# First two scans of a fused scan and two-MLP kernel: the order of ScalarE's fillers, the start of the second substitution, and the queue that loads the first MLP's x

## The chip, the cores and the metric

One Trainium2 chip, one core. The metric is the time of one execution on the device in microseconds (us), the median of several runs.

## What is computed

The reference runs a linear-attention scan with a state of 40 by 40 for each of 4 batches and 8 heads over 768 steps, and feeds its output through two MLPs:

```python
for t in range(S):                                   # S = 768, state: B=4, H=8, 40 x 40
    y[:, :, t] = np.einsum('bhd,bhde->bhe', rt, state)
    Sa = np.einsum('bhde,bhe->bhd', state, at)
    state_decay = state * wt[:, :, None, :] - np.einsum('bhd,bhe->bhde', Sa, bt)
    state = state_decay + np.einsum('bhd,bhe->bhde', vt, kt)
...
h = x @ w_in                                         # x: 3072 x 320, w_in: 320 x 2048
g = np.maximum(h, 0.0) + alpha * np.minimum(h, 0.0)
x = g @ w_out
...
g = x @ w_gate                                       # 320 x 1536
silu = g * (1.0 / (1.0 + np.exp(-g)))
out = (silu * (x @ w_val)) @ w_out
```

The MLP weights arrive as 8-byte floating point and are cut down to pairs of 4-byte parts on the chip.

## The kernel before

The 768 steps are cut into 6 blocks `m` of 128 steps, and a block into 2 chunks of 64. A pair (block, batch) is an item; there are 24, four to a block. Each item goes through these stages, all of them Python generators that yield after each step:

- `preps` (7 steps to an item): decayed copies of the inputs on DVE (`kbt` L592, `AN` L579, the running products L565 to L572), products `mnp` on PE, whose results ScalarE copies into the block's triangular matrices `tt` (L610, L613) and into `AN` (L617). The matrices of even blocks are `tt_172`, of odd ones `tt_173`; the number is the buffer's.
- `inverse(m)` (40 steps, once to a block): the triangular inverse of all four items' matrices, the substitution. DVE transposes `tt` (L650), runs 31 rounds of a product (L665) and a subtraction (L673), and transposes back (L676, L678). PE then makes the off-diagonal quarter in two sets of small products, `eps` (L686) and `dps` (L705); between and behind them stand ScalarE copies (L698, L694, L713). L650 needs the last L613 of the block.
- `seq(i, ch)` (13 steps to an item): the scan. For each chunk: `zp` on PE (L769), `zs` copied by ScalarE (L771), `pp` (L779, which needs the block's inverse), copies `ut` and `pv` (L781, L783), transposes, copies `gs` and `s` (L793, L798), `gp` on PE (L802), a masking on DVE (L805), `yp` on PE (L817, L821), and on DVE the state (L825), the output (L829) and the next chunk's start (L746). Two items run side by side on two channels. At its end ScalarE's queue writes the output to DRAM, `xd` (L837).
- `conv1` (32 steps): conversion of the first MLP's weights: a load `raw` on SP's queue, ScalarE (L191, L192, L217), DVE (L193), GpSimd (L218), a store to `wd`.
- `mlp1(m)`: the first MLP over a block. It loads x from `xd` into `xa` in three tiles (`fill_x`; L319 twice, L323 for the two halves of the third), splits it into high and low parts (ScalarE L217 or L324, DVE L218 or L325), and goes through 16 blocks of weights, `f`: 8 up products `u` (L294), ScalarE and DVE for the activation (L334, L335, L217, L218), 8 down products `d` (L300 to L306). For block 0 the first 8 weight blocks run over half of x (items 0 and 1) before the rest.

`drive` takes steps from several of these by their progress and gives each a priority; a list scheduler then puts the instructions of the whole program in one fixed order for each engine. An engine runs its own order strictly, and so does a queue: an instruction whose semaphores are not there holds up all behind it. DMAs of SP and of ScalarE share 8 completion semaphores, and a DMA waits until the one before it on its semaphore has landed. `tc.issue_after(ins)` orders what is traced under it behind `ins` on the same engine; `lifted(n)` raises the priority by `n`. In `drive` the first `lead` generators log the last instruction of their step on each engine; of the others, those that `who` names have their instructions ordered behind that log on the engines that `engs` names.

The part around the change: `preps` of block 0, then `inverse(0)`, then a first `drive` with the scans of items 0 and 1, the remaining 27 steps of `preps` of block 1, all of `inverse(1)` and the last 20 steps of `conv1`; then a second one with the scans of items 2 and 3 and 17 steps of `mlp1(0)`; then a loop over the other blocks, in which block `m` is scanned while block `m + 1` is prepared and inverted and block `m - 1` goes through the first MLP. The second MLP stands at the end.

Of the kernel before, what the change touches and what calls it, by code (L numbers as in the profile page):

```python
# [16 lines left out]
FAC = 1.0  # L17
ALIAS = 1
XPRI = 1000
# [26 lines left out]
RA = 1.0  # L46
MP = 0
YB = 1
CP = 2000
# [14 lines left out]
L = 64  # L64
HALF = 32
LOOK = 2
TRB = 5
LATE = 20
XLEAD = 6
# [4 lines left out]
def kernel(  # L74
# [50 lines left out]
    @contextmanager  # L125
    def held_by(ins):
        n0 = len(traced())
        yield
        if ins is not None:
            for x in traced()[n0:]:  # L130
                if x.engine == nc.sync.engine:
                    tc.add_manual_dep(
                        x, ins.ins.name,
                        mybir.DependencyInfo(mybir.DependencyClass.Sync, mybir.DependencyReason.DATA),
                        reason="pace of loads",
                    )
# [39 lines left out]
    @contextmanager  # L176
    def lifted(n=XPRI):
        tc.cur_priority -= n
        yield
        tc.cur_priority += n  # L180
# [130 lines left out]
        xst = pool.tile([128, n], F32R, tag="xst", name="xst")  # L311
        return xh, xl, xst

    def fill_x(pool, xs, src, c0, c1):
        xh, xl, xst = (x[..., c0:c1] for x in xs)
        for j in range(3):
            xa = pool.tile([128, c1 - c0], F32, tag="xa", name="xa", bufs=XAB[0])
            if j < 2:
                nc.sync.dma_start(out=xa, in_=src[j * 128:j * 128 + 128])  # L319
                split(xa, xh[:, j], xl[:, j], nc.vector)  # L320
            else:
                for p in (lo, hi):
                    nc.sync.dma_start(out=xa[p], in_=src[256:DM])  # L323
                nc.scalar.copy(out=xst, in_=xa)  # L324
                nc.vector.tensor_tensor(out=xst[hi], in0=xa[hi], in1=xst[hi].bitcast(F32), op=ALU.subtract)  # L325

# [31 lines left out]
    def mlp1(j, early=0):  # L358
# [15 lines left out]
        seen = set()  # L374
        for f, c0, c1 in plan:
            if not seen & {(c0, c1), (0, half) if early and c0 == 0 else (c0, c1)}:
                with lifted(), held_by(ago(XLEAD) if j == NM - 1 else None):
                    b0, b1 = c0 // TB, c1 // TB
                    fill_x(xp1, xs, xd[j][:, b0:b1].rearrange("f b t -> f (b t)"), c0, c1)
                seen.add((c0, c1))  # L380
                yield
            t = fetch(wp1, 2 * f, True, j, done)
            ps = e1p["psu"].tile([128, c1 - c0], F32, tag="u", name="u")
            done.append(up_mm(ps, t, tuple(x[..., c0:c1] for x in xs)))
            yield
            if len(pend) == (2 if j == NM - 1 else DEP):
                down(*pend.pop(0))
            pend.append((f, c0, c1, *prelu(e1p["gp3"] if j == NM - 1 and fs.index(f) % 3 == 2 else gp1, ps, f, c1 - c0)))
            yield
# [514 lines left out]
    if FA == 0:  # L904
        drive(
            *((chain(seq(j, j), seq(j + 2, j)), 2 * N_SEQ, SP) for j in range(2)),
            (rest1, FAC * nrest, HP2),
            (take(c1, NC1), NC1 - EC - EC0, CP),
            lead=2, engs=G1, lag=LG1, who=W1,
        )  # L910
    else:
        drive(
            (seq(0, 0), N_SEQ, SP), (seq(1, 1), N_SEQ, SP),
            (take(rest1, int(nrest * RA)) if RA < 1 else rest1, FAC * nrest, HP2),
            (take(c1, NC1), NC1 - EC - EC0, CP),
        )
    boot.close()
    ps1 = ctx.enter_context(ExitStack())
# [7 lines left out]
    if FA:  # L926
        drive(
            (seq(2, 0), N_SEQ, SP), (seq(3, 1), N_SEQ, SP),
            (rest1, FAC * nrest * (1 - RA) + .1, HP2),
            (take(gms[0], 2 * FA + 1), 2 * FA + 1, MP),  # L930
        )
    for m in range(1, NM):
# [201 lines left out]
```

## Time and profile before

| | |
|---|---|
| median of 3 runs | 1228.72 us (1226.75 to 1228.92) |
| profiled execution | 1225.27 us, its span 1223.6 us |
| mean granted clock of TensorE | 0.952 of full speed |
| busy in the span | PE 1107.1 us (90%), PEld 935.2, DVE 735.3 (60%), ACT 607.1 (50%), POOL 272.0 |
| chain that ended last | PE 29% of the span, as far back as it is followed |

PE is TensorE's products, PEld its weight loads, DVE VectorE, ACT ScalarE, POOL GpSimd; SPq and ACTq are the queues that issue DMAs. Times in rows are us from the span's start unless marked ns. In a timeline row stand the start, the duration, the engine, the line, what it writes and reads, the form, how many equal ones are merged, and in brackets the idle time before it and what ended it. In a row of windows stand the stretch, its length, the busy time and in brackets the instructions of PE, PEld, DVE, ACT and POOL, the granted clock of TensorE, the busy share of the DMA engines and GB/s.

### The profile page before, as it was taken

To read this page: it belongs to the slowest core of one execution; us is meant where nothing else is said; L and a number is where in the kernel's file an instruction comes from. 1 tells how busy PE (TensorE), PEld (TensorE's weight loads), DVE (VectorE), ACT (ScalarE), POOL (GpSimd) and SP (SyncE) were. 2 spreads that over 40 slices of the span, in tenths; PEclk is the share of its full clock that TensorE was granted. 3 is DMA by queue.
4 is the path that set the end of the run, shared out by engine and by line. 5 is a ranking of instruction groups with operands and counts; after the bars stand their busy time and mean duration, and the time that the engine had idled before them with its cause. 6 is when DMAs were issued, how large, how long until landed. Compare 5 with 4: busy or idle time off the path is not lost. (4 is left out here: it accounts for less than half of the span.)

```text
span 1223.6 us, 24425 instructions
## 1 busy us (share of the span) xinstructions
PE 1107.1 (90%) x9098; PEld 935.2 (76%) x9098; DVE 735.3 (60%) x1592; ACT 607.1 (50%) x1514; POOL 272.0 (22%) x434
## 2 busy tenths in 40 slices
PE   4566678999999989899898999999999999999998
PEld 3345567877878778787686777788788888888887
DVE  7787897698499569859664434879532323223222
ACT  5769658645844764673654433555332323222222
POOL 8115333301212221521363000536300000000000
PEclk9659787999999999899989999999999999999999
DMA  4565697466454544545585473795010101010000
GB/s 145 179 198 176 210 310 228 138 200 185 132 170 137 170 140 148 181 133 147 160 269 189 129 221 135 261 351 158 1 48 1 48 1 48 2 39 9 22 1 21
DMA packets 94884, 166.35 MB, mean 136 GB/s; under 512 B 13232, under 2 KB 43184, under 8 KB 94768
## 3 DMA queue, kind: packets, MB, share of 16 engines
q1 hardware_dynamic: 86608, 160.88, 41.8%
q10 hardware_dynamic: 8160, 3.93, 1.1%
q8 instruction: 72, 1.18, 0.4%
q14 instruction: 44, 0.36, 0.1%
HBM read 136.98 MB, written 27.79 MB: 135 GB/s over the span
## 5 line engine op out<-in xcount | busy, mean ns | idle before, releaser
L217 ACT CAST gh<-g 128x512 fp32r<-128x512 f32 (+1 forms) x176 | 105.5, 600 | 165.0 <-DVE g L1070 115.9
L218 DVE TENSOR_TENSOR gl<-g,gh 128x512 fp32r<-128x512 f32 (+1 forms) x176 | 124.2, 706 | 89.5 <-ACT gh L217 87.1
L1070 DVE TENSOR_TENSOR g<-pv,sg 128x512 f32<-128x512 f32 x72 | 49.8, 691 | 206.3 <-PE pv L294 201.6
L294 PE MATMUL u<-xh,wt 128*128 128x512 f32 (+1 forms) x416 | 147.4, 397 | 11.9 <-DVE g L335 11.0
L335 DVE SCALAR_TENSOR_TENSOR g<-g,neg,u 128x512 f32<-128x512 f32 (+1 forms) x104 | 72.8, 702 | 70.4 <-ACT g L334 69.8
L294 PEld LDWEIGHTS u<-xh,wt 128*128 128x128 f32 x416 | 79.7, 194 | 31.4 <-DVE g L335 14.3
L1068 ACT ACTIVATE sg<-pg 128x512 f32<-128x512 f32 x72 | 43.1, 598 | 121.1 <-PE pg L294 121.1
L294 PE MATMUL pg<-xh,w 128*128 128x512 f32 x288 | 102.5, 394 | 0.0
L294 PE MATMUL pv<-xh,w 128*128 128x512 f32 x288 | 100.4, 389 | 0.0
L334 ACT ACTIVATE g<-u 128x512 f32<-128x512 f32 (+1 forms) x104 | 58.6, 564 | 82.7 <-PE u L294 69.9
L1054 PE MATMUL o<-w,gh 128*128 128x320 f32 x288 | 87.5, 309 | 2.6 <-ACT gh L217 2.6
L1055 PE MATMUL o<-w,gh 128*128 128x320 f32 x288 | 87.8, 309 | 0.0
L301 PE MATMUL d<-gl,wt 128*128 128x512 f32 (+1 forms) x208 | 83.2, 402 | 2.2 <-DVE gl L218 2.2
L604 PE MATMUL mnp<-AN,kbt 128*128 128x128 f32 x384 | 60.1, 307 | 25.6 <-DVE AN L579 13.6
L665 DVE TENSOR_TENSOR tmp<-la 128x96 f32<-128x96 f32 (+43 forms) x306 | 79.5, 286 | 2.7 <-POOL la L653 0.7
L294 PE MATMUL u<-xl,wt 128*128 128x512 f32 (+1 forms) x208 | 80.2, 385 | 0.0
L302 PE MATMUL d<-gh,wt 128*128 128x512 f32 (+1 forms) x208 | 79.9, 386 | 0.0
L1056 PE MATMUL o<-w,gl 128*128 128x320 f32 x288 | 77.2, 310 | 1.0 <-DVE gl L218 0.9
L673 DVE TENSOR_TENSOR la<-la,tmp 128x96 f32<-128x96 f32 (+43 forms) x306 | 76.8, 277 | 2.0
L760 POOL COPY gs<-raw_v 64x160 f32<-64x160 f32 x96 | 43.3, 451 | 148.8 <-PE yp L817 72.2
L618 POOL TENSOR_SCALAR_AFFINE_SELECT AN<-AN 64x256 f32<-64x256 f32 x96 | 50.2, 523 | 117.9 <-ACT AN L617 98.4
L604 PEld LDWEIGHTS mnp<-AN,kbt 128*128 128x128 f32 x384 | 53.4, 214 | 30.0 <-DVE AN L579 13.6
(129 smaller groups left out, 2630.1 us busy)
## 6 DMA issues: line engine op xcount, KB each, us to landing
wt<-wd SPq DMA_DIRECT2D x98, 384.0 KB
wt<-wd SPq DMA_DIRECT2D x98, 320.0 KB
wd<-wc SPq DMA_DIRECT2D x24, 384.0 KB
raw<-in_moe_w_out_dram SPq DMA_DIRECT2D x28, 320.0 KB
raw_bk<-in_bk_dram SPq DMA_DIRECT2D x48, 160.0 KB
wd<-wc SPq DMA_DIRECT2D x20, 320.0 KB
raw<-in_moe_w_in_dram SPq DMA_DIRECT2D x16, 256.0 KB
raw_v<-in_v_dram SPq DMA_DIRECT2D x24, 160.0 KB
```

The costliest lines, as they stand in the source:

```text
L217: nc.scalar.copy(out=h, in_=raw)
L218: eng.tensor_tensor(out=l, in0=raw, in1=h.bitcast(F32), op=ALU.subtract)
L294: last = nc.tensor.matmul(ps, lt, rh, start=(i == 0), stop=(i == len(ops) - 1))
L301: nc.tensor.matmul(ps, wh, gl, start=False, stop=False)
L302: nc.tensor.matmul(ps, wl, gh, start=False, stop=last)
L335: nc.vector.scalar_tensor_tensor(g, g, neg[:, f:f + 1], ps, ALU.mult, ALU.add)
L604: nc.tensor.matmul(ps[:, s].rearrange("p h t -> p (h t)"), kbt[:, g * SH + s].rearrange("p j t -> p (j t)"), an[:, :, g * SH + s, :],)
L665: nc.vector.tensor_tensor(out=tv, in0=ml[:, kk + 1:HALF, kk:kk + 1].to_broadcast([128, nr, ns]), in1=tl[:, kk:kk + 1, c0:c0 + ns].to_broad ...
L673: mark["inv"] = nc.vector.tensor_tensor(out=dst, in0=dst, in1=tv, op=ALU.subtract)
L1054: nc.tensor.matmul(ops[q], gh[:, ts], wh, start=first, stop=False)
L1055: nc.tensor.matmul(ops[q], gh[:, ts], wl, start=False, stop=False)
L1056: nc.tensor.matmul(ops[q], gl[:, ts], wh, start=False, stop=last)
```

## The change

Three things are done to the stretch of the first four scans.

1. In the first `drive`, the fillers (`preps` of block 1 and `conv1`) are ordered on ScalarE behind the last ScalarE instruction that a step of one of the two scans has logged (`lead=2, engs=4, lag=1, who=3`; `engs=4` is ScalarE alone).
2. `inverse(1)` and 12 of the last 20 steps of `conv1` are given out in the second `drive`, beside the scans of items 2 and 3, and not in the first.
3. The x of block 0, both halves, is loaded on ScalarE's queue, and with a priority lifted by 6000 where it was 1000.

```diff
@@ -64,6 +64,7 @@
 LOOK = 2
+FIRST = 6000
 TRB = 5
@@ -311,16 +312,16 @@
-    def fill_x(pool, xs, src, c0, c1):
+    def fill_x(pool, xs, src, c0, c1, eng=nc.sync):
...
-                nc.sync.dma_start(out=xa, in_=src[j * 128:j * 128 + 128])
+                eng.dma_start(out=xa, in_=src[j * 128:j * 128 + 128])
...
-                    nc.sync.dma_start(out=xa[p], in_=src[256:DM])
+                    eng.dma_start(out=xa[p], in_=src[256:DM])
@@ -374,9 +375,9 @@
-                with lifted(), held_by(ago(XLEAD) if j == NM - 1 else None):
+                with lifted(XPRI if j else FIRST), held_by(ago(XLEAD) if j == NM - 1 else None):
...
-                    fill_x(xp1, xs, xd[j][:, b0:b1].rearrange("f b t -> f (b t)"), c0, c1)
+                    fill_x(xp1, xs, xd[j][:, b0:b1].rearrange("f b t -> f (b t)"), c0, c1, nc.sync if j else nc.scalar)
@@ -911,8 +912,9 @@
             (seq(0, 0), N_SEQ, SP), (seq(1, 1), N_SEQ, SP),
-            (take(rest1, int(nrest * RA)) if RA < 1 else rest1, FAC * nrest, HP2),
-            (take(c1, NC1), NC1 - EC - EC0, CP),
+            (take(rest1, 27), 27, HP2),
+            (take(c1, 8), 8, CP),
+            lead=2, engs=4, lag=1, who=3,
         )
@@ -926,7 +928,8 @@
             (seq(2, 0), N_SEQ, SP), (seq(3, 1), N_SEQ, SP),
-            (rest1, FAC * nrest * (1 - RA) + .1, HP2),
+            (rest1, nrest - 27, HP2),
+            (take(c1, NC1), NC1 - EC - EC0 - 8, CP),
             (take(gms[0], 2 * FA + 1), 2 * FA + 1, MP),
         )
```

No instruction is added or taken away, but for the engine that issues eight loads. Since one scheduler orders the whole program, the order shifts from here up to the last scan. In the new file each line below the first insertion has a number one higher (L650 is L651, L319 is L320). Three places carry most of it.

**ScalarE, up to the last copy that the second substitution waits for.** The rows are ScalarE's in program order; `tt_173` is the matrix of block 1, and the last L613 of it releases L650. Before:

```order
L613 COPY tt_173<-mnp 32x4x32 x2
L617 COPY AN<-mnp 64x256 x2
L217 CAST wc<-wz 128x256
L217 CAST wc<-wz 128x64
L192 ACTIVATE wy<-raw 128x384
L191 ACTIVATE wz<-raw 128x384
L771 COPY zs_164<-zp 64x4x40 x2
L771 COPY zs_168<-zp 64x4x40 x2
```

The same copy of the changed kernel, with what stands around it:

```order
L794 ACTIVATE gs<-pp 64x2x2x40 x2
L799 COPY s_1380<-pp 128x256
L611 COPY tt_173<-mnp 64x256 x4
L636 COPY KB<-kbp 128x320 x2
L192 ACTIVATE wz<-raw 128x320
L193 ACTIVATE wy<-raw 128x320
L614 COPY tt_173<-mnp 32x4x32
L192 ACTIVATE wz<-raw 128x384
L614 COPY tt_173<-mnp 32x4x32
L618 COPY AN<-mnp 64x256 x2
L614 COPY tt_173<-mnp 32x4x32 x2
L618 COPY AN<-mnp 64x256 x2
```

Ahead of that last copy stood one chunk of both scans, and now stand both chunks: four copies `zs`, two `ut` with two `pv` each, two pairs `gs` with an `s` each, and one L191 of the conversion have moved in front of it; behind it, where the second chunk's `zs` stood, now stands the write of item 0's output.

**VectorE, at the start of the second substitution.** Before, the second chunk of both scans lay inside it:

```order
L746 TENSOR_TENSOR gs<-ST_176,Wx 64x2x2x40 x2
L650 STREAM_TRANSPOSE la<-tt_173 128x1024
L193 SCALAR_TENSOR_TENSOR wz<-wz,wy 128x384
L665 TENSOR_TENSOR tmp<-la 128x31
L665 TENSOR_TENSOR tmp<-la 128x21
L673 TENSOR_TENSOR la<-la,tmp 128x31
L673 TENSOR_TENSOR la<-la,tmp 128x21
```

In the changed kernel:

```order
L806 TENSOR_TENSOR gs<-gp,mask 128x8x64
L194 SCALAR_TENSOR_TENSOR wz<-wz,wy 128x320
L747 TENSOR_TENSOR gs<-ST_180,Wx 64x2x2x40 x2
L651 STREAM_TRANSPOSE la<-tt_173 128x1024
L826 TENSOR_TENSOR ST_176<-yp,ST_176 128x4x40
L830 TENSOR_TENSOR pv<-yp,Wx 128x2x2x64
L194 SCALAR_TENSOR_TENSOR wz<-wz,wy 128x384
L573 SCALAR_TENSOR_TENSOR Wx<-wseg,first 128x520
L576 MEMSET first 128x4
L580 TENSOR_TENSOR AN<-raw_a_142,Wx 128x1024
L666 TENSOR_TENSOR tmp<-la 128x31
```

Four L746, two L805, one L825 and one L829 have moved from inside the substitution (L650 to L676) to ahead of it; one L218 and two L335, the first MLP's, have moved in. The large L572 and L579 of the next item stood eight rounds into it and now stand ahead of its first round.

On PE, between the first `eps` of block 0 and the first `eps` of block 1, stood six up blocks and five down blocks of the first MLP (8 products each), and now stand eight and six; the products of scan and preparation are the same number there.

**The queues that load x.** Before, SP's rows around the x of items 0 and 1:

```order
L547 DMA raw_vt_159<-in_vt_dram 40x512 x2
L512 DMA raw_a_142<-in_wa_dram 40x512 x2
L511 DMA raw_w_134<-in_wa_dram 40x512 x2
L319 DMA xa<-xd_57 128x256 x2
L323 DMA xa<-xd_57 64x256
L244 DMA raw<-in_moe_w_in_dram 128x2x256
L547 DMA raw_vt_159<-in_vt_dram 40x512 x2
L264 DMA wd<-wc 128x640
L246 DMA raw<-in_moe_w_in_dram 64x256 x2
L249 DMA raw<-in_moe_w_out_dram 128x640
L264 DMA wd<-wc 128x768
L323 DMA xa<-xd_57 64x256
```

In the changed kernel these four loads stand in ScalarE's order:

```order
L193 ACTIVATE wy<-raw 128x320
L192 ACTIVATE wz<-raw 128x320
L782 COPY ut<-pp 128x256
L320 DMA xa<-xd_57 128x256 x2
L324 DMA xa<-xd_57 64x256
L218 CAST xh<-xa 128x256
L324 DMA xa<-xd_57 64x256
L218 CAST xh<-xa 128x256
L738 COPY pv<-raw_vt_159 128x2x2x64 x2
L784 ACTIVATE pv<-pp 128x2x64 x2
```

The four loads have left a queue on which eight other DMAs stood between the first and the last of them, and stand almost together among ScalarE's own work. The other half of x, of items 2 and 3, stands on ScalarE directly ahead of the copies that follow the second substitution; before, only two `pv` copies stood in that place:

```order
L335 ACTIVATE g<-u 128x256
L320 DMA xa<-xd_57 128x256 x2
L324 DMA xa<-xd_57 64x256 x2
L738 COPY pv<-raw_vt_159 128x2x2x64 x2
L192 ACTIVATE wz<-raw 128x384
L699 COPY tt_173<-tt_173 32x32x32 x2
```

L699 (L698 before) works on the result of L678, and the four loads and their waits now lie in front of it.

## Rows read from the trace of the kernel before

**Rows 1.** Windows by stage; columns as told under the profile before.

```profile
81.00:121.00 40.00, 31.04 (x441) 27.21 (x437) 32.64 (x51) 38.01 (x107) 20.87 (x29) 0.85 0.51 157
121.00:186.00 65.00, 47.17 (x624) 41.52 (x624) 58.29 (x165) 38.60 (x121) 24.18 (x44) 0.82 0.80 265
186.00:200.00 14.00, 9.44 (x171) 8.70 (x168) 11.30 (x18) 12.69 (x29) 5.40 (x7) 0.58 0.78 249
286.00:386.00 100.00, 96.82 (x991) 79.48 (x984) 78.18 (x197) 66.15 (x180) 19.35 (x40) 1.00 0.53 161
```

**Rows 2.** Timeline of ScalarE, 110 to 130 us.

```profile
110.96 0.61 ACT L793 ACTIVATE gs<-pp 64x160 f32<-64x160 f32 x2
...
112.48 0.37 ACT L798 COPY s<-pp 128x256 f32<-128x256 f32 x1
...
122.79 1.18 ACT L771 COPY zs<-zp 64x160 f32<-64x160 f32 x4
...
125.28 0.37 ACT L781 COPY ut<-pp 128x256 f32<-128x256 f32 x1
...
126.13 0.49 ACT L783 ACTIVATE pv<-pp 128x128 f32<-128x128 f32 x2
...
129.37 0.55 ACT L191 ACTIVATE wz<-raw 128x384 f32<-128x384 f32 x1
```

**Rows 3.** Timeline of VectorE over the second substitution, 120 to 186 us.

```profile
120.79 1.97 DVE L650 STREAM_TRANSPOSE la<-tt 128x1024 f32<-128x1024 f32 x1 [0.62 <-ACT tt L613]
...
128.62 0.49 DVE L193 SCALAR_TENSOR_TENSOR wz<-wz,wy 128x320 uint32<-128x320 uint32 x1 [2.24 <-ACT wz L191]
...
130.35 0.69 DVE L805 TENSOR_TENSOR gs<-gp,mask 128x512 f32<-128x512 f32 x1 [0.97 <-PE gp L802]
...
183.66 1.91 DVE L678 STREAM_TRANSPOSE tt<-la 128x1024 f32<-128x1024 f32 x1
```

**Rows 4.** VectorE's groups by form, 81 to 186 us: count, busy, mean ns, idle.

```profile
L746 DVE TENSOR_TENSOR gs<-ST,Wx 64x160 f32<-64x160 f32 x16 | 5.8, 362 | 0.2
L805 DVE TENSOR_TENSOR gs<-gp,mask 128x512 f32<-128x512 f32 x8 | 5.5, 684 | 5.8 <-PE gp L802 5.8
L829 DVE TENSOR_TENSOR pv<-yp,Wx 128x256 f32<-128x256 f32 x8 | 3.3, 409 | 0.0
L335 DVE SCALAR_TENSOR_TENSOR g<-g,neg,u 128x256 f32<-128x256 f32 x5 | 2.4, 471 | 0.3 <-ACT g L334 0.3
```

**Rows 5.** Timeline of SP's queue: the first and the last load of x.

```profile
145.18 0.82 SPq L319 DMA_DIRECT2D xa<-xd  x2
...
152.60 0.52 SPq L323 DMA_DIRECT2D xa<-xd  x1
```

**Rows 6.** Timeline of ScalarE and its queue, 134 to 187 us.

```profile
134.95 0.86 ACTq L837 DMA_DIRECT2D xd<-pv  x2
...
141.76 0.71 ACT L737 COPY pv<-raw_vt 128x256 f32<-128x256 f32 x2 [3.87 <-DMA raw<-in_moe_w_out_dram]
...
155.90 0.40 ACT L324 CAST xst<-xa 128x256 fp32r<-128x256 f32 x1 [1.14 <-DMA xa<-xd]
...
178.77 0.70 ACTq L837 DMA_DIRECT2D xd<-pv  x2
...
182.93 0.71 ACT L737 COPY pv<-raw_vt 128x256 f32<-128x256 f32 x2 [1.89 <-DMA xd<-pv]
...
185.60 2.11 ACT L698 COPY tt<-tt 32x1024 f32<-32x1024 f32 x2 [1.96 <-DVE tt L678]
```

**Rows 7.** Timeline of TensorE: first and last rows of two up blocks.

```profile
166.48 0.28 PE L294 MATMUL u<-xh,wt 128*128 128x256 f32 x1
...
167.20 0.40 PE L294 MATMUL u<-xst,wt 128*128 128x256 f32 x2
...
188.69 0.58 PE L294 MATMUL u<-xh,wt 128*128 128x256 f32 x1 [2.65 <-DVE g L335]
...
190.13 0.63 PE L294 MATMUL u<-xst,wt 128*128 128x256 f32 x2
```

## The prediction

> **What bounds the kernel now.** I read the windows by stage first, since one mean hides that the stages have different limits. In the loop over the blocks TensorE is the bound: from 286 to 386 us it is busy 96.82 of 100 us at full clock, and VectorE 78 [rows 1]. In the stretch that the change touches it isn't. From 81 to 121 us ScalarE is busy 38.01 of 40 us and TensorE 31; from 121 to 186 us VectorE is busy 58.29 of 65 us and TensorE 47.17, at a granted clock of 0.82, that is, partly at 1.2 GHz; from 186 to 200 us TensorE is busy 9.44 of 14 us at 0.58 [rows 1]. So the start is a chain of two waits: ScalarE makes the matrices of block 1, then VectorE inverts them.
>
> The timelines show the two joints. The second substitution starts at 120.79 us, released by ScalarE's last copy of the matrix, L613; it ends with the transpose L678, from 183.66 to 185.57 us [rows 3]. Then ScalarE's L698 starts at 185.60, after an idle wait of 1.96 us for that transpose: ScalarE is 2 us ahead there [rows 6]. The scan of block 1 can't pass this point, and behind it TensorE is nearly saturated. So I price the change as two numbers: by how much the end of the second substitution moves, and how much of TensorE's work moves from behind it to ahead of it. Their sum goes to the end of the program almost one to one.
>
> **ScalarE's fillers and the second substitution's start.** Ahead of ScalarE's last copy for the substitution now also stands the second chunk of both scans. From the rows of such pieces: four copies `zs`, 1.18 us; two sets of `ut` and `pv`, from 125.28 to 126.62, 1.34 us; two sets of `gs` and `s`, from 110.96 to 112.85, 1.89 us; one L191 of the conversion, 0.55 us [rows 2]. Together 5.0 us, and ScalarE was 95% busy, so nothing hides them. The steps of a scan also follow each other more closely now, each with a trip through TensorE or VectorE between. No row shows that wait in the new place; the nearest is VectorE's for `gp`, 0.97 us [rows 3]. Bounds are nothing and twice that; I take 0.5. The start moves by +5.5 us (5.0 to 6.9), to 126.3 us.
>
> **VectorE inside the substitution.** The second chunk has left it: four L746 at 0.362, two L805 at 0.684, one L829 at 0.409 us, together 3.2 us (the shorter L825 I leave out). Three small instructions of the first MLP move in, priced by L335 at 0.471, so 1.4 us [rows 4]. That is -1.8 us. Two idle waits go with the chunk: 2.24 us for ScalarE's L191, which stood behind scan steps, and 0.97 us for `gp` [rows 3]. Their instructions now stand before the start, so I count -3.2 us; the bound on the other side is 0, if the conversion's next L193 waits as long. The next item's L572 and L579 change place, not number, and cost nothing in the sum.
>
> **x from ScalarE's queue.** On SP the first load of x started at 145.18 us and the last at 152.60, 7.4 us later, because weight loads stood between, which wait for their own buffers [rows 5]. The last tile was used at 155.90 after an idle wait of 1.14 us, 3.3 us after its issue [rows 6]. On ScalarE the four loads stand together, but behind item 1's write, and VectorE's split now stands early in the substitution, so its wait has to be priced. How long a write takes to land has two rows: from 179.47 (the issue's end) to 182.93, where L737 had waited 1.89 us for it, 3.5 us; and from 135.81 to 141.76, 5.95 us, if that wait of 3.87 us was for the write, whose buffer L737 takes, and not for the weight load that the row names [rows 6]. I take 3.5, since the row names the write itself. Then ScalarE ends item 0's write at 127.2 (126.3 and 0.86), gets past its landing at 130.7, has done L737 and the copies at about 132.1, item 1's write at 132.9, its landing at 136.4, and the first part of x is in after 3.3 us and split on ScalarE at about 140.1. VectorE comes to its split at about 138.9, an estimate: the start of 126.3, 1.97 for L650 [rows 3], and some 10.6 for six rounds of the substitution, the two large instructions that now stand ahead of them and a few pieces of scan and conversion. So the substitution waits 1.2 us (nothing to 6.1: each landing of 5.95 adds 2.45).
>
> The Trainium skill speaks against this part. Its page "DMA: Bandwidth & Descriptors", section "Issuing engines are not separate DMA queues", says that DMAs started by different engines run on the same 16 DMA engines, and that a second issuing engine saves only the sequencer's time for the issue. By it x would come no earlier. The rows show something else that is saved, the 7.4 us of order on SP; no run here shows yet whether it is had. What the rule would make of the time is a rival below.
>
> **TensorE's work brought forward.** The new order has two more up blocks and one more down block of the first MLP ahead of the substitution's first `eps`. An up block took from 166.48 to 167.60, 1.1 us, at full clock, and from 188.69 to 190.76, 2.1 us, in the stretch of clock 0.58; that second block is one of those that move [rows 7]. A down block has eight products of the same size. So 2.1 + 1.1 + 1.1 = 4.3 us of TensorE's time lies ahead of the joint and not behind it. The bound is 2.2 us, if the block at 188.69 had filled a hole that stays one.
>
> **The sum.** End of the substitution: +5.5 - 1.8 - 3.2 + 1.2 = +1.7 us. Work brought forward: -4.3 us. Together -2.6 us. The profiled execution took 1225.27 us around a span of 1223.6, so it would take 1222.7; it lies 3.45 us below the median of the runs shown, 1228.72, so on that scale I forecast **1226.1 us**. A measurement of this kernel can tell about 0.2%, 2.5 us, from no change, so this is just faster.
>
> **The rivals.**
> - *VectorE stops waiting (larger gain).* VectorE was idle 6.7 us from 121 to 186 [rows 1], of which the sum takes 3.2. If the other 3.5 and the wait for x go too, because conversion and scans no longer alternate on ScalarE, it is -2.6 - 3.5 - 1.2 = -7.3 us, 1221.4. Against it: the conversion has as many L193 inside the substitution as before.
> - *One slow landing (no change).* If one of the two writes lands in 5.95 us, the split waits 2.45 us more: -0.2 us, 1228.5. For it: that row is the one with the same neighbours, weight loads in flight.
> - *x comes no earlier (the change doesn't do its work; no change).* As a mechanism here: x waits on ScalarE for landings and for the loads that hold its completion semaphores, as long as it did on SP. Then the blocks brought forward wait too, their 4.3 us are lost, and what is left is +1.7 us, 1230.4. This is the case in which the skill's rule decides.
> - *The second half of x holds up the joint (slower).* Its four loads stand on ScalarE directly ahead of L698, behind item 3's write. That write started at 178.77, 6.8 us before L678 ended [rows 3, 6]. With a landing of 5.95 us it is in at 185.4; four issues, two of 0.82 and two of about 0.5 each, 1.8 us; L737 and an L191, 1.3 us [rows 2, 5, 6]; so L698 would start at 188.5 and not 185.6, +2.9 us. If writes land that slowly, the first half has two of them, +4.9. Together -2.6 + 7.8 = +5.2 us, 1233.9. It decides from about +5 us on, since the rest must first be eaten up. Against it: ScalarE's 2 us of slack there, and the landing of 3.5 us, which is that of this very write.
>
> **How the numbers follow.** The forecast has 0.30, the larger gain 0.12, one slow landing 0.20, x no earlier 0.13, the slow joint 0.25. The forecast and the larger gain are faster by over 0.2%: 0.42. The two cases with no change: 0.33. The last one: 0.25. The range takes in the larger gain and, below it, the start moved by only 5.0 and no wait at all in the rounds; above, the slow joint with the copies' wait at 1.9: 1217.5 to 1235 us. Without the cases of the other sign the forecast's own range is 1223 to 1228.
>
> **What would show it.** In the changed kernel's profile: the second substitution's L650 near 126 us, released by ScalarE's copy as before; L678 ending near 187; `xa` issued from ScalarE near 136 to 138 us, and the last tile used some 12 us earlier than 155.90; eight up blocks ahead of the first `eps` of block 1; L698 still released by VectorE and not by a DMA. The prediction is wrong if L698 waits for a DMA, if VectorE's first split of x waits more than 4 us, if L650 starts where it did, or if the loop behind 200 us gains or loses by its own new order: it has some 4% of idle TensorE, which the sum takes as unchanged.

## The result, and the profile after

The changed kernel takes **1237.40 us** (median of 4 runs, 1235.01 to 1239.54) against 1227.74 us of the kernel before in the same set (1224.44 to 1228.92): ratio **1.0074**, 95% interval 1.0051 to 1.0098, 9.7 us slower. The forecast was 1226.1 us, the range 1217.5 to 1235. The profiled executions are 1237.43 and 1225.27 us, spans 1235.7 and 1223.6, so the traces have 12.1 us to explain; the one of before is a short one among its own runs.

The changed kernel's page, its head, busy times and TensorE's clock in 40 slices:

```profile
span 1235.7 us, 24427 instructions
PE 1118.7 (91%) x9098; PEld 945.3 (76%) x9098; DVE 736.3 (60%) x1592; ACT 607.8 (49%) x1514; POOL 274.0 (22%) x434
PEclk9658796999999998998999999999999999999999
```

TensorE does the same 9098 products and is idle as long as before (1235.7 - 1118.7 = 117.0 us; 116.5 before). Nearly all of the 12.1 us stands in busy time: +11.6 us, at a mean granted clock of 0.941 of full speed where it was 0.952. Span times clock is 1162.8 us after and 1164.9 before, 0.2% apart: as much work, at a lower clock. That the idle sum is equal hides an exchange, though, and the windows by stage (columns as in [rows 1]) show where:

```profile
81.00:121.00 40.00, 31.28 (x509) 27.74 (x510) 28.31 (x44) 33.06 (x93) 15.74 (x24) 0.80 0.44 141
121.00:186.00 65.00, 48.10 (x497) 42.59 (x496) 57.32 (x164) 44.45 (x135) 25.81 (x48) 0.83 0.80 259
186.00:200.00 14.00, 10.40 (x228) 9.32 (x228) 12.09 (x22) 8.27 (x18) 4.07 (x5) 0.57 0.85 289
286.00:386.00 100.00, 94.22 (x1012) 77.05 (x1009) 73.57 (x173) 61.73 (x164) 19.91 (x46) 0.97 0.53 156
```

Against [rows 1], ScalarE has lost its dense stretch from 81 to 121 us (33.06 busy for 38.01), and TensorE is no longer full from 286 to 386 us: 94.22 us at 0.97 where it was 96.82 at full clock. The first comes with the tie and the late giving out together: in the same window ScalarE is busy 37.75 us with the late giving out and no tie (`no_tie`), 36.67 with the tie alone (`tie_only`) and 33.59 with both (`order_only`). The second lies 90 us behind the last instruction that the change names.

For the comparisons the span is cut at L678, the last transpose of a substitution (L679 in the new numbering). In these sums what lies ahead of the third L678 counts as the front, and the stretch from there to the span's end is the rest; in the experiments the front is the order of the first four scans, and the loop all that is traced behind them. The starts are:

| | second L650 | second L678 | third L678 | from there to the span's end |
|---|---|---|---|---|
| before | 120.8 | 183.7 | 284.9 | 938.7 us |
| changed | 131.8 | 190.9 | 289.9 | 945.8 us |
| difference | +11.0 | +7.2 | +5.0 | +7.1 |

So 5.0 of the 12.1 us are lost in the front and 7.1 behind it. Up to the last scan the loss behind the front is 11.5 us (419.4 and 430.9 us, windows in set 3); 4.4 are back in the second MLP, since 2499 of TensorE's products are left behind the last scan where it was 2516. Of the 5.0, 2.2 were there at the first L679, which starts at 81.43, and at 79.2 before; up to 87 us VectorE, ScalarE, TensorE and SP's queue have the same order in both. Executions of one order differ by as much there: five with the front of before up to there (before, its two nudges, `before_loop_of_after` and `x_only`) start it at 78.2 to 81.5, and four with that of the changed kernel at 81.2 to 82.1. So the 2.2 us can be chance.

**The start of the second substitution.** Windows from one L678 to the next L650, before and after:

```profile
79.20:120.80 41.60, 32.45 (x492) 28.77 (x492) 34.24 (x52) 38.30 (x108) 20.67 (x28) 0.84 0.49 152
```

```profile
81.40:131.80 50.40, 40.26 (x612) 35.98 (x612) 36.15 (x59) 42.86 (x124) 19.76 (x32) 0.82 0.47 148
```

The stretch is 8.8 us longer. ScalarE is busy 4.56 us longer, for the second chunk of both scans (forecast 5.0), and idle 7.54 us, not 3.30 (forecast +0.5). Its timeline in the changed kernel, the waits in brackets:

```profile
98.30 0.37 ACT L782 COPY ut<-pp 128x256 f32<-128x256 f32 x1 [1.50 <-PE pp L780]
100.05 0.65 ACT L561 COPY wseg<-raw_w 128x512 f32<-128x512 f32 x1
115.13 0.55 ACT L218 CAST wc<-wz 128x256 fp32r<-128x256 f32 x2 [1.07 <-DVE wz L194]
117.61 0.21 ACT L577 COPY Wx<-rest 128x8 f32<-128x8 f32 x1 [1.18 <-DVE Wx L573]
131.52 0.26 ACT L614 COPY tt<-mnp 32x128 f32<-32x128 f32 x1
```

A filler behind a scan step inherits the step's wait: `wseg` of `preps`, at 87.81 us before, now stands behind `ut`, which waits for TensorE, and starts at 100.05. VectorE's next instruction, which needs it, waits:

```profile
100.74 1.29 DVE L566 TENSOR_TENSOR_SCAN rest<-wseg,first 128x260 f32<-128x260 f32 x2 [5.38 <-ACT wseg L561]
```

Of ScalarE's 4.2 us of new idle time, 1.7 are waits for the scans' products (L782, 1.50, and L794, 0.23 at 125.31) and 2.3 are waits of fillers for VectorE (L218 and L577).

**x, and the second joint.** ScalarE's and VectorE's timelines further on:

```profile
131.46 0.28 ACTq L838 DMA_DIRECT2D xd<-pv  x1
137.22 0.71 ACT L738 COPY pv<-raw_vt 128x256 f32<-128x256 f32 x2 [3.14 <-DMA xd<-pv]
142.47 0.36 ACTq L320 DMA_DIRECT2D xa<-xd  x1
145.73 0.46 ACTq L324 DMA_DIRECT2D xa<-xd  x1
145.73 0.41 ACT L218 CAST xh<-xa 128x256 fp32r<-128x256 f32 x1 [2.78 <-DMA xa<-xd]
150.05 0.40 ACT L325 CAST xst<-xa 128x256 fp32r<-128x256 f32 x1 [0.73 <-DMA xa<-xd]
186.83 3.07 ACTq L320 DMA_DIRECT2D xa<-xd  x2
189.95 1.41 ACTq L324 DMA_DIRECT2D xa<-xd  x2
191.40 0.71 ACT L738 COPY pv<-raw_vt 128x256 f32<-128x256 f32 x2 [5.28 <-DMA wt<-wd]
192.85 2.11 ACT L699 COPY tt<-tt 32x1024 f32<-32x1024 f32 x2 [0.28 <-DVE tt L679]
```

```profile
131.81 1.95 DVE L651 STREAM_TRANSPOSE la<-tt 128x1024 f32<-128x1024 f32 x1 [1.27 <-ACT tt L614]
142.72 0.62 DVE L194 SCALAR_TENSOR_TENSOR wz<-wz,wy 128x320 uint32<-128x320 uint32 x1 [2.43 <-ACT wz L192]
146.17 0.42 DVE L219 TENSOR_TENSOR xl<-xa,xh 128x256 fp32r<-128x256 f32 x1
190.93 1.89 DVE L679 STREAM_TRANSPOSE tt<-la 128x1024 f32<-128x1024 f32 x1
```

x is there earlier although the substitution starts later: its last tile at 150.05 us, not 155.90. ScalarE pays for it in waits for landings, and what stands behind them makes VectorE wait 2.43 us. From L651 to L679 it is 59.1 us and was 62.9. Ahead of L699 ScalarE issues the four loads of the other half of x, which hold it until 191.4, but L679 still comes last: 0.28 us of its 2 us of slack are left.

### The profile page after: what moved, and what is told of

Same layout as the page of the kernel before. It is cut to its first block, busy times and chain, and to the rows that moved or that the text cites. A ratio compares the mean times of both kernels' runs of the same rounds, so it can differ in the third digit from the quotient of the medians.

```text
span 1235.7 us, 24427 instructions
## 1 busy us (share of the span) xinstructions
PE 1118.7 (91%) x9098; PEld 945.3 (76%) x9098; DVE 736.3 (60%) x1592; ACT 607.8 (49%) x1514; POOL 274.0 (22%) x434
## 4 chain that ended last, share of the span: by engine, by line
PE 62%; DVE 14%; DMA 9%; ACT 9%; issue 4%; POOL 1%; SPq 1%; ACTq 0%; DVEq 0%; POOLq 0%
PE u L295 11%; PE pv L295 10%; PE pg L295 10%; PE o L1059 3%; PE o L1058 3%; PE o L1057 3%; PE d L301 3%; PE d L302 3%; PE mnp L605 2%; PE d L303 2%; PE gp L803 2%; DMA xd<-pv 2%; PE yp L818 2%; DVE la L674 2%; DVE tmp L666 2%
## 5 line engine op out<-in xcount | busy, mean ns | idle before, releaser
L218 ACT CAST gh<-g 128x512 fp32r<-128x512 f32 (+1 forms) x176 | 105.5, 601 | 165.3 <-DVE g L1073 116.0
L219 DVE TENSOR_TENSOR gl<-g,gh 128x512 fp32r<-128x512 f32 (+1 forms) x176 | 121.7, 691 | 89.3 <-ACT gh L218 87.0
L295 PE MATMUL u<-xh,wt 128*128 128x512 f32 (+1 forms) x416 | 152.3, 409 | 11.0 <-DVE g L336 7.5
L336 DVE SCALAR_TENSOR_TENSOR g<-g,neg,u 128x512 f32<-128x512 f32 (+1 forms) x104 | 72.8, 701 | 78.8 <-ACT g L335 78.5
L295 PEld LDWEIGHTS u<-xh,wt 128*128 128x128 f32 x416 | 82.3, 201 | 31.9 <-DVE g L336 12.0
L335 ACT ACTIVATE g<-u 128x512 f32<-128x512 f32 (+1 forms) x104 | 58.6, 564 | 93.3 <-PE u L295 74.9
L295 PE MATMUL pg<-xh,w 128*128 128x512 f32 x288 | 102.4, 393 | 0.0
L666 DVE TENSOR_TENSOR tmp<-la 128x96 f32<-128x96 f32 (+43 forms) x306 | 76.6, 275 | 3.0 <-POOL la L654 1.2
```

The costliest lines, as they stand in the source:

```text
L218: nc.scalar.copy(out=h, in_=raw)
L219: eng.tensor_tensor(out=l, in0=raw, in1=h.bitcast(F32), op=ALU.subtract)
L295: last = nc.tensor.matmul(ps, lt, rh, start=(i == 0), stop=(i == len(ops) - 1))
L336: nc.vector.scalar_tensor_tensor(g, g, neg[:, f:f + 1], ps, ALU.mult, ALU.add)
L666: nc.vector.tensor_tensor(out=tv, in0=ml[:, kk + 1:HALF, kk:kk + 1].to_broadcast([128, nr, ns]), in1=tl[:, kk:kk + 1, c0:c0 + ns].to_broad ...
```

## Experiments

Theories: **A**, the end of the second substitution and TensorE's work ahead of it set the time, as the prediction has it; **B**, ScalarE's queue holds it up; **C**, the new order of the loop costs the time, though no instruction of it was touched; **D**, a fixed order fits only the front it was worked out with; and for the front's rest F1 to F3, below. Ratios are to runs of before in the same set; the times of L678 come from one profiled execution of each kernel.

**1. One part alone, or one part less.** `x_only` has the diff's parts on `fill_x` alone, `order_only` the two `drive` calls alone; `tie_only` adds one line to before, and `no_tie` takes it from the changed kernel:

```diff
-            lead=2, engs=4, lag=1, who=3,
```

> Only the third part of the change: x of block 0 is issued on ScalarE with the priority lifted by 6000; the fillers and the second substitution are given out as before. Theory A (the late start of the second substitution is the loss): the start depends on ScalarE's order ahead of the last copy of the matrix, which is that of the kernel before, so the second substitution starts near 121 us (131.8 in the changed kernel) and the time is that of before, 1225 to 1230 us. Theory B (ScalarE's queue is the loss, because ScalarE stops for landings and for x, 3.14 and 2.78 us in the changed kernel): 1232 us or more, with a late end of the second substitution. Theory C (the loop's new order is the loss, and TensorE's granted clock of 0.50 behind its waits there): the front is as in A, and the stretch from the end of the third substitution to the last scan differs from the 419 us of before by 3 us or more, in either direction; 1222 to 1238 us.

> The first and the second part without the third: fillers tied and the second substitution given out late as in the changed kernel, x loaded on SP as before. Theory A: the second substitution starts near 132 us, as in the changed kernel; three up blocks fewer of the first MLP stand ahead of the substitution's first small products (5 and not 8), so the time is 1237 to 1242 us. Theory B: with ScalarE free of x and its landings the loss is gone, 1231 us or less. Theory C: late start as in A, but the stretch from the end of the third substitution to the last scan differs from the 431 us of the changed kernel by 3 us or more.

> The changed kernel without the tie: the second substitution is given out late and x is loaded on ScalarE, but the fillers are not ordered behind the scan steps. ScalarE's order ahead of the last copy of the matrix has one chunk of both scans, as before, and not two. Theory A: the second substitution starts near 121 to 124 us, 8 to 11 us earlier than in the changed kernel, and of this 7 us stay at its end, so 1229 to 1232 us; four up blocks fewer ahead of its small products can take 4 us of that back. Theory B: ScalarE's queue still stops for landings, 1235 us or more. Theory C: the front gains as in A, and the stretch from the end of the third substitution to the last scan goes its own way by 3 us or more against 431 us.

> The kernel before with the tie alone: fillers ordered on ScalarE behind the scan steps in the first two scans, the second substitution and all conversion steps given out in the first stretch as before, x on SP. ScalarE's order ahead of the last copy of the matrix has one chunk of both scans, as before. Theory A: the second substitution starts near 121 us; what is lost is only that fewer up blocks stand ahead of its small products (2 and not 6), 4 to 8 us, so 1231 to 1236 us. Theory B: as before, 1225 to 1230 us. Theory C: the stretch from the end of the third substitution to the last scan differs from the 419 us of before by 3 us or more, whatever the front does.

| | time, us | ratio (interval) | second L650 | second L678 | third L678 | rest |
|---|---|---|---|---|---|---|
| x_only | 1242.84 | 1.0094 (1.0065 to 1.0124) | 123.3 | 185.2 | 288.8 | 953.1 |
| order_only | 1238.56 | 1.0063 (1.0043 to 1.0084) | 130.2 | 188.5 | 289.5 | 947.1 |
| no_tie | 1232.69 | 1.0018 (1.0004 to 1.0033) | 123.2 | 176.3 | 290.4 | 939.0 |
| tie_only | 1246.44 | 1.0122 (1.0105 to 1.0139) | 121.7 | 178.5 | 286.7 | 959.4 |

The late start needs the first two parts together, as A said: only there do two chunks stand ahead of the last copy. A's time holds in `order_only` alone (1238.56 us for 1237 to 1242); it misses by 0.7 us in `no_tie` and by over 10 us in the other two. Two kernels end the second substitution 5 to 7 us earlier than before and are slower (`no_tie` by 0.18%, `tie_only` by 1.22%); `x_only` ends it 1.5 us later and is slower by 0.94%. Only in `order_only` does what is lost at the second L678 (4.8 us) stand at the third (4.6), and the rest varies by 20 us. What C said of the stretch from the third L678 to the last scan holds in all four (427.8 and 431.2 us in `x_only` and `tie_only`, against 419; 423.9 and 414.1 in `order_only` and `no_tie`, against 431), though `x_only` takes longer than C's 1238 us. B falls with `order_only`. The parts don't add up either: alone they cost 12.5 us (x) and 16.1 us (tie), together with the late giving out 9.7.

**2. The front untouched, one number of the loop's pace changed.** The weight that spreads the preparation of the next block over one pass goes from 68 to 67, for pass 1 or pass 2:

```diff
-FAC * (B * N_PREP + N_INV), HP))
+FAC * (B * N_PREP + N_INV) - (m == 1), HP))
```

> The kernel before, with one number changed in the loop: the steps that prepare and invert the next block count as 67 and not 68 in the pace of the first pass of the loop. The order of every engine is the same up to about 210 us, and nothing is added or left out. Theory A (the end of the second substitution and the work ahead of it set the time): nothing changes, 1227 to 1232 us, and the stretch from the end of the second substitution to the last scan stays at 521 us. Theory C (each order of the loop has TensorE waits of its own, with a granted clock of 0.50 behind some of them): that stretch changes by 3 us or more, and since before has one of the shorter ones so far, rather upward: 1231 to 1242 us.

> The same nudge in the second pass of the loop, so that the order is that of before up to about 390 us. Theory A: 1227 to 1232 us, the stretch from the end of the fourth substitution to the last scan stays at 320 us. Theory C: that stretch changes by 2 us or more; 1229 to 1240 us.

> The changed kernel with the nudge in the first pass of the loop: the same order as the changed kernel up to about 215 us, so the second substitution starts near 132 us and ends near 191 us as there. Theory A: 1236 to 1240 us, as the changed kernel. Theory C: the 530 us from the end of the second substitution to the last scan change by 3 us or more, in either direction; 1228 to 1245 us.

> The changed kernel with the nudge in the second pass of the loop. Theory A: 1236 to 1240 us. Theory C: the 322 us from the end of the fourth substitution to the last scan change by 2 us or more, in either direction; 1230 to 1243 us.

| | time, us | ratio (interval) | second L678 | third L678 | rest |
|---|---|---|---|---|---|
| before_nudge1 | 1248.14 | 1.0151 (1.0114 to 1.0187) | 186.9 | 285.5 | 961.8 |
| before_nudge2 | 1229.80 | 1.0012 (0.9989 to 1.0034) | 184.5 | 284.8 | 941.3 |
| after_nudge1 | 1232.48 | 1.0034 (1.0015 to 1.0054) | 192.1 | 291.9 | 938.0 |
| after_nudge2 | 1240.40 | 1.0099 (1.0063 to 1.0135) | 192.0 | 291.4 | 947.3 |

An edit that means nothing in particular costs before 20 us, twice what the change under study costs; the same nudge makes the changed kernel 5 us faster (1.0034 for 1.0074, with intervals that barely overlap). A is out for the larger part, C stands. By time the nudge in pass 2 shows nothing: `before_nudge2` can't be told from before, nor `after_nudge2` from the changed kernel. In `after_nudge2` the stretch from the fourth L678 to the last scan did move as C said, by 7 us, but the time didn't follow.

**3. Fronts and loops exchanged.** All instructions that are traced from the loop on (the first MLP's, the scans', the second MLP's; without the four loads of x's second half) get their order on each engine from a list, that of before or of the changed kernel. The front stays free:

```diff
+    loop0 = len(traced())
     for m in range(1, NM):
...
+            for p, n in zip(seq, seq[1:]):
+                tc.add_manual_dep(
+                    every[first + n], every[first + p].name,
+                    mybir.DependencyInfo(mybir.DependencyClass.NoSync, mybir.DependencyReason.DATA),
```

In the traces the order of every engine and queue behind some 210 us is that of the kernel whose list was used, but for one or two neighbouring records.

> The changed kernel with the order of before in the loop: each engine's instructions from the loop on (blocks 1 to 5 and what follows, but for the four loads of the second half of x) are chained in the order that they have in the kernel before; the first four scans keep the order of the changed kernel. Theory C (the loop's new order is the larger part of the loss): the stretch from the end of the third substitution to the last scan goes back from 431 us to 419 to 423 us, and only the front's part stays, 1230 to 1234 us. Theory A (the front sets it): 1236 to 1240 us. Theory D (a fixed order suits only the front that it was worked out with): no gain, 1236 us or more, with new waits in the first pass of the loop.

> The reverse: the first four scans in the order of before, the loop and what follows chained in the order of the changed kernel. Theory C: the front of before with the loop's loss, 1232 to 1238 us, and 428 to 432 us from the end of the third substitution to the last scan. Theory A: as before, 1227 to 1231 us. Theory D: worse than both, 1238 us or more.

> The third part of the change alone (x on ScalarE's queue, priority lifted), with the loop in the order of before. Theory C: what this part cost when the loop was free to change (1242.8 against 1230.4 us) goes but for what its own front loses, up to 3 us: 1228 to 1233 us. Theory A or B (the part itself costs it): 1238 us or more. Theory D: 1234 us or more.

> The second substitution given out late and x on ScalarE's queue, without the tie, with the loop in the order of before. In the run without the fixed loop the second substitution ended at 176.3 us, 7 us earlier than in before, with four up blocks fewer (2 to 3 of 64 us of TensorE's work each) done by then than in the changed kernel. Theory C: 1226 to 1231 us. Theory A (the end of the second substitution goes to the end one to one): 1221 to 1224 us. Theory D: 1234 us or more.

| | time, us | ratio (interval) | second L678 | third L678 | rest |
|---|---|---|---|---|---|
| after_loop_of_before | 1232.70 | 1.0019 (0.9997 to 1.0041) | 191.9 | 294.3 | 943.1 |
| before_loop_of_after | 1248.24 | 1.0150 (1.0123 to 1.0178) | 185.3 | 298.9 | 945.9 |
| x_loop_of_before | 1236.81 | 1.0056 (1.0035 to 1.0076) | 184.2 | 294.2 | 939.1 |
| no_tie_loop_of_before | 1237.24 | 1.0061 (1.0040 to 1.0081) | 177.9 | 295.1 | 939.9 |

The changed kernel with the loop of before stands at 1.0019, not 1.0074, and the intervals don't meet, as C expected: most of the loss is the loop's order. What its front loses by this, 0.19%, isn't clear of no change. Its profile is the longest of its 12 executions (1239.15 us, the median 1232.70), so its own L678s can lie some us late. The order carries its time along: the stretch from the third L678 to the last scan, in windows of before, `after_loop_of_before`, the changed kernel and `before_loop_of_after`, in this order:

```profile
284.90:704.30 419.40, 390.40 (x4308) 324.22 (x4309) 297.01 (x708) 251.82 (x669) 114.00 (x196) 0.97 0.54 164
```

```profile
294.30:716.60 422.30, 391.65 (x4307) 324.78 (x4308) 297.66 (x707) 251.47 (x669) 113.57 (x196) 0.97 0.54 163
```

```profile
289.90:720.80 430.90, 398.62 (x4318) 330.51 (x4318) 299.65 (x710) 251.23 (x668) 116.11 (x196) 0.96 0.53 160
```

```profile
298.90:728.60 429.70, 397.93 (x4318) 330.23 (x4318) 300.08 (x709) 251.84 (x668) 115.90 (x196) 0.96 0.53 161
```

419 and 422 us against 431 and 430. Over before and the six other fronts of sets 3 and 4 with its order it is 418 to 422 us. C's time holds for `after_loop_of_before` alone, though, and D's for the other three; what D names lies in another place: where front and loop come from different kernels, the stretch from the second to the third L678 grows: 113.6 us in `before_loop_of_after` (101.2 in before), 110.0 in `x_loop_of_before` (103.6 in `x_only`), 117.2 in `no_tie_loop_of_before` (114.1 in `no_tie`), 102.4 in `after_loop_of_before` (99.0 in the changed kernel). So the front of before with the other loop is slower than either kernel.

The waits themselves travel. TensorE's timeline at one place of the second pass, the changed kernel and then the front of before with the changed kernel's loop (lines 113 higher):

```profile
361.50 0.39 PE L307 MATMUL d<-gl,wt 128*128 128x512 f32 x1
364.04 0.69 PE L780 MATMUL pp<-tt,zs 128*64 128x64 f32 x16 [2.16 <-ACT zs L772]
364.66 0.50 PE L295 MATMUL u<-xh,wt 128*128 128x512 f32 x1
```

```profile
367.87 0.39 PE L420 MATMUL d<-gl,wt 128*128 128x512 f32 x1
371.36 0.69 PE L893 MATMUL pp<-tt,zs 128*64 128x64 f32 x16 [3.10 <-ACT zs L885]
371.97 0.50 PE L408 MATMUL u<-xh,wt 128*128 128x512 f32 x1
```

A down block ends, the next instruction is a scan's `pp` whose `zs` isn't there, and the next up block stands behind it. In before an up block and three products of a down block lie between the two scans' `pp` at this step, and the waits are 0.59 and 0.54 us:

```profile
350.27 0.69 PE L779 MATMUL pp<-tt,zs 128*64 128x64 f32 x16 [0.59 <-ACT zs L771]
351.49 0.50 PE L294 MATMUL u<-xh,wt 128*128 128x512 f32 x1 [0.54 <-DVE g L335]
354.21 0.69 PE L779 MATMUL pp<-tt,zs 128*64 128x64 f32 x16
```

Waits of TensorE over 1.5 us from 285 to 725 us: 4 in before (9.6 us together), 9 in the changed kernel (22.8 us), 10 in `before_loop_of_after` (22.5 us), 5 in `after_loop_of_before` (11.9 us); over the seven fronts with the order of before, 2 to 7 (6.1 to 15.0 us). It isn't only TensorE's order: of eight of the nine (the other is an up block's own), in four the next up block could not have run before the wait ended, since L336, which frees its buffer, ended later still.

**4. The front alone, with the loop held in the order of before.** Open was what makes the front's rest: the late start (F1), x on ScalarE (F2), or the join with a loop worked out for another front (F3). `late_only` is `order_only` without the tie.

> Tie and late giving out together, x on SP, with the loop in the order of before. Theory F1 (the late start makes the front's loss): the second substitution starts near 130 us and the time stays where the changed kernel with this loop order is, 1231 to 1234 us. Theory F2 (x on ScalarE's queue makes it): 1228 to 1230 us. Theory F3 (the join: a fixed loop order waits for up blocks that the front has not done; this front has 5 of them ahead of the second substitution's small products, before has 6, the changed kernel 8): the stretch from the end of the second to the end of the third substitution is 105 us or more and the time 1234 us or more.

> The tie alone, with the loop in the order of before. Theory F1: no late start, so 1228 to 1232 us. Theory F2: the same, since x is on SP. Theory F3: only 2 up blocks stand ahead of the small products, so the stretch from the end of the second to the end of the third substitution is 112 us or more (101 in before) and the time 1236 us or more.

> The late giving out alone, with the loop in the order of before. Theory F1 and F2: 1228 to 1232 us. Theory F3: 4 up blocks ahead of the small products, between before and the tie alone: that stretch 106 to 115 us, the time 1233 to 1238 us.

| | time, us | ratio (interval) | second L678 | third L678 | second to third | rest |
|---|---|---|---|---|---|---|
| order_only_loop_of_before | 1243.49 | 1.0106 (1.0077 to 1.0136) | 189.5 | 301.5 | 112.0 | 939.9 |
| tie_only_loop_of_before | 1243.30 | 1.0122 (1.0093 to 1.0150) | 177.5 | 302.4 | 124.9 | 938.4 |
| late_only_loop_of_before | 1236.08 | 1.0052 (1.0034 to 1.0071) | 177.9 | 289.6 | 111.7 | 939.1 |

F3's numbers hold in all three, for the stretch and for the time, and the times of F1 and F2 miss in all three. By up blocks done ahead of the small products, sets 3 and 4 with before give a stretch of 124.9 us for 2, 117.2 and 111.7 for 4, 110.0 and 112.0 for 5, 101.2 for 6 and 102.4 for 8. So the stretch goes with the count, but the count isn't all of it: with 4 it differs by 5.5 us, and the stretch is longer also because the second L678 comes earlier (177.5 us with 2 blocks done, 191.9 with 8). F1 can't be separated from the join by these runs.

What x on ScalarE does depends on the rest of the front. With tie and late giving out it is faster by 0.9% (`after_loop_of_before` 1.0019, third L678 at 294.3, against `order_only_loop_of_before` 1.0106, 301.5). Without the tie it can't be told from x on SP (`no_tie_loop_of_before` 1.0061, 295.1, against 1.0052, 289.6, in the shortest of that kernel's executions), and alone it costs 0.56%. The tie with x, without the late giving out, wasn't run. So with the loop held, each part alone and both pairs that were run cost 0.5 to 1.2%, and only all three together can't be told from before.

Counted over before and sets 3 and 4, seven fronts with one loop order give a rest of 938.4 to 943.1 us; two with the changed kernel's give 945.8 and 945.9. The difference of the means is 6.1 us. Holding the order costs nothing visible there: the rest is 938.7 us in before, where nothing is held.

No version here is faster than before.

## Why the prediction was wrong

In the profiled execution, term by term (the sum was made against that time):

- **Start of the second substitution: +5.5 forecast, +8.8 measured** beside the 2.2 us of the execution. Mechanism right (released by ScalarE's copy, two chunks ahead of it), the work too (4.56 for 5.0). Mis-sized was the wait of tied fillers: 0.5 us taken, from VectorE's wait for `gp`, and 4.2 found. That row was one wait of one engine; tied fillers wait with ScalarE's scan steps (1.7 us), and then ScalarE waits for VectorE's part of the fillers (2.3), which had itself waited for ScalarE.
- **Inside the substitution: -3.8 forecast (-1.8, -3.2, +1.2), -3.8 measured** (62.9 to 59.1 us). The sum agrees, partly by luck: the wait came at a conversion step (2.43 us), which the forecast had put at nothing and named as the bound on the other side, and not at the split of x, where 1.2 us were forecast. No row stood behind the 10.6 us from L650's end to that split; it took 12.4 us with that wait, and 10.0 without. The last tile of x came 5.9 us earlier, where 12 was forecast.
- **Work brought forward: -4.3 forecast, -2.2 by the only measure there is**: what of the +7.2 at the second L678 is back at the third. The eight up blocks are there; why no more came back was not tested.
- Together +5.0 (2.2 of it can be the execution's) where the sum had **-2.6**.
- **Loop: 0 forecast, +7.1 measured.** This step failed: "behind it TensorE is nearly saturated", so that the sum "goes to the end of the program almost one to one", with an idle share "which the sum takes as unchanged". The prediction named the loop's own order among what would make it wrong and gave it no price. In place of an unchanged idle share stand nine waits of TensorE over 1.5 us where there were four, and 37.5 us at half clock where there were 23.9. It is the larger part of the loss: shown by the exchange of loops (1.0074 to 1.0019), and that a new order alone can cost so much by the 20 us of a nudge with the front untouched.

The point where the prediction read the time doesn't hold either: the second L678 moved from 176 to 192 us over these kernels without the time following it. How many blocks of the first MLP are done ahead of the joint matters too: the stretch behind the joint goes with it (set 4).

The rivals: x came earlier, so "x comes no earlier" is out. The Trainium skill's rule on it (page "DMA: Bandwidth & Descriptors", section "Issuing engines are not separate DMA queues", that a second issuing engine saves only the issue's time) does not decide here. The last tile was used 5.9 us earlier with the loads on ScalarE, and from the first load to the last it is 3.3 us (142.47 to 145.73) where it was 7.4 on SP: what was saved is mostly the place behind SP's other loads. Slow landings are there: the first write's issue ended at 131.74 and L738 was let go at 137.22, 5.5 us, near the 5.95 us of that rival and far from the 3.5 us of the forecast. The slow joint missed by 0.28 us, and its total, 1233.9, came nearest to the time by luck, for a reason that wasn't its own. The range's lower end doesn't follow from what is named for it (1221.4 less 0.5 is 1220.9, not 1217.5); the time lies beyond the upper end.

What stays open: how much of the front's loss is the late start and how much the join, and how much of it is clear of the spread between executions. Why one order of the loop has more waits than another was followed at one place only. Whether keeping TensorE busy in its waits would keep its clock was not tried.

## What to carry to other kernels

Where one scheduler orders a whole program, an edit of one stage is two edits: the one meant, and a new draw of every order behind it. Price the second from the start, as a spread and not as zero: a few neutral nudges of the pace give an idea of its size (four here, from nothing to 20 us), and one part alone measures mostly that draw. To see an edit's own worth, hold the order behind it fixed, and look at the stretch where the two meet, since a fixed order also has to fit what the front leaves done. Here the parts couldn't be priced one by one even so.

## What the runs showed of the hardware

A wait of TensorE can cost more than itself, since a stretch at half clock often follows. Such a wait in the changed kernel, and windows ahead of it, right behind it, and later:

```profile
311.33 0.69 PE L788 MATMUL pp<-ident,ut 128*128 128x128 f32 x2 [3.12 <-ACT pv L784]
```

```profile
304.00:308.00 4.00, 4.00 (x46) 3.28 (x42) 3.93 (x6) 1.44 (x3) 0.00 (x0) 1.00 0.92 284
311.00:314.00 3.00, 2.67 (x8) 2.20 (x9) 1.08 (x2) 2.87 (x12) 0.82 (x2) 0.50 0.68 207
315.00:319.00 4.00, 4.00 (x30) 3.60 (x28) 3.06 (x4) 2.90 (x10) 0.21 (x1) 1.00 0.36 114
```

After the wait the granted clock is 0.50 (1.2 GHz), and then full again. Of the nine waits over 1.5 us in the changed kernel's loop, eight have such a stretch within 5 us of their end; of four in before, two, and there three of the five such stretches have no wait over 1.5 us that near. From 285 to 730 us these stretches add up to 23.9 us in before and in `after_loop_of_before` (17.1 to 27.3 over the seven fronts with the order of before), and to 37.5 us in the changed kernel and in `before_loop_of_after`: the clock that is lost goes with the order too. The 13.6 us more at half clock are 6.8 us of full clock; that is most of the 8.2 us by which TensorE's busy time from the third L678 to the last scan grew (390.40 to 398.62, with ten more products).

Also unexpected: executions of one order differ by up to 3.3 us in the first 80 us (78.2 to 81.5), as much as the terms of the sum, which was made against one execution 3.45 us below the median.
